# Moving weight loads to GpSimd, u's copy to TensorE, and the last output in two parts, in a planned RWKV-and-MLP kernel

## The chip, the cores and the metric

The kernel runs on one core of a Trainium2 chip. A core has five engines that the texts name as the profile does: PE (TensorE, the matrix engine, with its weight loads as PEld), DVE (the vector engine), ACT (ScalarE), POOL (GpSimd) and SP (which only begins transfers). ACT and POOL can begin transfers too. The core's transfers are carried by 16 DMA engines. The metric is the device time of one execution in microseconds, and the kernel before is given by the median of three of them. "Span" is the time from the first to the last instruction of the one execution that was profiled.

## The reference

Two blocks follow each other. The first is a linear attention with a state of 48x48 per head (4 batches, 8 heads, 768 steps), the second a dense layer with the activation h - tanh(h):

```python
for t in range(S):
    cur = einsum('bhd,bhe->bhde', u[None] * kt, vt)
    y[:, :, t] = einsum('bhd,bhde->bhe', rt, state + cur)
    state = w[None, :, :, None] * state + einsum('bhd,bhe->bhde', kt, vt)
x = y.transpose(0, 2, 1, 3).reshape(3072, 384)
h = x @ w_in            # 384 -> 2048
out = (h - tanh(h)) @ w_out   # 2048 -> 384
```

The inputs r, k, v, w and u are float32, w_in and w_out are float64, which the kernel loads as 64-bit integers and converts to float32 itself. The output is 3072x384 float32.

## The kernel before

**Units.** The sequence is cut into 12 chunks of 64 steps, and each chunk into two halves of two batches: 24 units, each with 128 rows (2 batches by 64 steps) by 8 heads of 48. A unit (`unit(n)` inside `lay_out`) loads r, k and v (two transfers each of 96 KB, begun by SP, for units 0 and 1 half of them by ACT), turns r and k with TensorE (`turn`), scales them by powers of w (`scale_r`, `scale_k`, or `copy_k`), multiplies them into levels (`levels`), masks these into `at` (a predicated copy, L830), forms outputs (`outputs`) and updates the state (`to_state`, `keep`, `decay`). Unit 0 takes u into its levels (`own_k`, `own_levels`); from unit 1 on, the vector engine forms r * k * u (`own`, and L824 with `ub`, a copy of u on all 128 partitions) and its sum `du`. A unit's result goes into `xt` (`to_xt`); a third of it passes through a tile `rest`, from which GpSimd copies it into `xt` by six small transfers per pair of units (`fill`, L786).

**Dense tiles.** Two units make one group of 256 columns, j = 0 to 11. For each group the 2048 hidden numbers are worked through in steps of two times 128 (`hidden`, f = 0, 2, ... 14): `Dense.h` computes h for two blocks of 128 (L217), ACT and the vector engine apply the activation, and `Dense.o` multiplies by w_out (L254), with a form of 7 products in place of 8 for many tiles (`products`, L307, with sums on GpSimd, L290 to L294). The first six groups go in three passes over f; the last six in one, and the last tile of all (group 11, f = 14) is a pass of its own, which ends the kernel: two times `Dense.o`, two adds into `last` (`empty`, L265 and L267), and four transfers to the output at the very end (L1247), two by SP and two by ACT, 96 KB each.

**Weights.** Sixteen pieces (`Weights`): of every four, two of w_in (384 KB of raw numbers in four transfers, 288 KB twice and 96 KB twice) and two of w_out (768 KB in one). Four staging buffers hold raw numbers, so piece n waits until piece n - 4 is converted. In the kernel before, SP begins the large parts and GpSimd the 96 KB parts. Each piece is converted by seven instructions, five on the vector engine (L185 to L191) and two on ACT. Tiles with f = 0 and 2 need pieces 0 and 1 for h and 2 and 3 for o.

**Order.** Nothing is scheduled at run time. `Plan.add` numbers every task in the order in which `lay_out` adds it, and the string `ORDER`, two digits per task in base 64, gives the order in which they are written; each engine then works through its own in that order and waits by semaphores. Numbers behind the last task stand for fills (`fills`, L534): matmuls of the identity whose results nobody reads, put where TensorE would stand idle, and for reading a flag. The first numbers of `ORDER` give TensorE two long fills, the transpose of the columns of w and u (`cols`, L549), two fills more, and then unit 0.

**The start.** w and u come by two small transfers into `rows`. TensorE turns them into columns, the vector engine makes the powers of w and their inverses (L554, L558), and TensorE and ACT make `w_down` from them (L529, L562). `ub` is loaded by one transfer of SP that reads u once for each of the 128 partitions (L568).

Of the kernel before, what the change touches and what calls it, by code (L numbers as in the profile page):

```python
# [10 lines left out]
F32 = mybir.dt.float32  # L11
# [4 lines left out]
ALU = mybir.AluOpType  # L16
# [12 lines left out]
C = 128  # L29
# [5 lines left out]
OWN = 1  # L35
SWAP = 2
# [21 lines left out]
    "AxLo1KLpLqAbB51XB6AoBFA+B71YB8BABG1Z1n1aBT1oBIBJBBAc2G2HBHL31p2FB9L4BUAdBMBKBCBf1bBWAeL5BVAp1cBYBXBNBgBLBaBbAqBi"
    "LTBh1dA_7S23241q2526B01rMABO1sKSKTB1BtBk1yBj1z1tBuB2Bm1+1uBD1_1vBZBE1wBlBvBcBPBy20KxBxBQBwKyKzBnBz2PB_2EC327B+28"
    "C4Bo29BRCH2A21C7BSCIC52BC6C0BdCK22CJCACLBe2XC82CM9MBCMCTCOC92ICN2DBp2J2QBq2RBr2SCUCPMf2TLzMgMhCBChCWCCCVBsCYCiCQ"  # L60
    "CXKdCbC1N3L+CZN4N52UC2CkCj2VCmCDCl2W2KCaCE2LCoCnCt2M2NCuCcD5CFCxCpCwCvCqD6CyCGC+CRD82OD7CzDK2Y2Z2aDL2bCSD92cDADC"
    "CdDBDDC_DZCfDM2dDNCe2eDaCgDECrD0DcDODFCsDbDRDGDdDPDgDoDQ85De86DpDfDS7rD1DrDhDq87EEDTD3DsDUDiEFDtDVDvD2EHDH81DuDW"
    "89ETEIDjEGELEJEUD4DkEK88EiDwEW8AEVDxDIEXEYDJDXEaDy7sDlEjEMENExEk8BElLUEmEy8CEZLVEnEbDYEoEqEzDmEpEOEcEPFNErE_DzE+"
    "FOF0EQF1D+F3DnFQ82FPD_F2EdFSE1EeFTE2FcF4EfFRE3E4E0FdE5EsE6EtE7ERE8FeEBFfE9FUFhESEuFVFgEDFrECFWF5FjEgF6FsEhFtFvEv"
    "FwFXFuFzFYFiEw7zFxEAG4FyF7FZFkG5Fl83F8FmG684G9FnG8F9F+G7FAGWGB7+FBGXFCFDFEFaFFGYGaFGFKGbGlGCGAFLGZF_FbGdFoGmGeGD"
    "FpFHGnFIGqG0G+GoGcG1FMGpG_GfGE7_FqGFH2GsH0FJG280H1GgGtGrG3GGH3H4GhGHGiGJGKGIGLGMHDGNGOGPHEGQGTGSH6GjK5GuH5HHGvGk"
    "HFH7GwHIHfHGGxHJHKH8HgK4H9GVGyHiHAHhHkGzHjHBHlHnHLKVHuK8HvHmK7I7HxHwI8HMKUHyHNHCH_IAHOHzHPHQH+I0HoKEI1IBHpI9IEIM"
    "ICHqKYGRINHrIFLPGUIoKFIOIQKXIDKGIRIPHRIUL6ITIpK+IGISHSIHKHJ1HTHUIIIVI2KIJ2HVIqKJIJIrHsHWL7HXK_HYHtJ4IsKeJ5IWIvIt"
    "IXIuJGKfI3J3I4L1J6I5LOJ7HZIwJHHbJ8HaIxI6JIL2JLKgJJLuJKKKL0JVLWHcJNJMHeJWJ9IyKhJAIKHdKiLQLMJOLXILKmLvKjIzJZL_IZI+"
# [12 lines left out]
    "VJOHWOVqNyWDVrOgOIWCWBP5WPVKVLVMVfVOWQVNW4WEOJVgW5WHVsVuOfOKVtWSORVvWGP6OOOLOQWdP7OMVQP0VRWTW7OPWRW6WFW8WIWeWVWJ"
    "WKOmWfOSWgWLWhVPWsP1WtOnP2OoWvWkWMOpWWWNWUOqWXX5WuWYWwP8WiWZWzWjWaONX6WxP9WlWbX8WmWyW+WnX9PAX7XCW_WcPBXVPCXAXWPD"
    "PIPFXkXYWoXZPHXBWpXlXcPEXXXDX0XzXnXaWqXbXdXEWrXoXFXmX3XGXpX1XqXsXHX+XrX2XtPGYCY0XeX_Y2XfX4Y1YDY4XuY5XgXIYGXvYFXh"
    "XKYRYJYEXwYHY3XJYKYIXLYSXMXNYLXiY6YTYVY7YgYUYWYYYXXOYhXPXSXQXRYvY8YjXTYkY9YiXjYlXxYmYnYMYZXUYwYNYaYOYoXyYxYzYpZ8"
    "YyYbZ0Z9YcYdYAZBY+ZCZYZ1ZAZDYBY_ZZZFYqZ2YrZnZGZcYsZbYPZEZaZHZdYQZeZoZfZ3Z4YeZpZ5ZqZrYfZsa0ZtZuZIZvZJYtZwZgYuZhZ6"
    "Zia1aFa2a5aGa4a3a6a7Z7aJa8aIaUZxaMZyZLZzZKZNZjZOaVa9ZkZPZMZQaXaHZlZRaAaKZSaLZVaNajaYZUaOaWaBabaZakaCZTZWZmalanZ+"
    "aaaPamZXayaQaqaRacazadbIa+b0a_Z_bJb3aeafaDagbLaoapaEarb1asaSb2bKaTbNbMahbObPb4aib5atawb6aubQavaxb7bRb9b8bBbCbAbD"
    "bEbSbFbGbHbUbTbV"
# [104 lines left out]
class Dense:  # L194
# [16 lines left out]
    def h(self, t, z):  # L211
        d = self.d
        if z == 0:
            t.h2 = self.ps_d.tile([128, 2, d.NT], F32, name="h", tag="h")
            t.h = t.h2.rearrange("p z t -> p (z t)")
        for kk in range(d.NK):
            self.nc.tensor.matmul(t.h2[:, z], self.w_in_sb[:, t.f // 2, kk, z * 128 : (z + 1) * 128],  # L217
                                  self.xts[t.j][:, kk].rearrange("p b t -> p (b t)"),
                                  start=kk == 0, stop=kk == d.NK - 1)
# [28 lines left out]
    def o(self, t, half):  # L248

        if t.first and half == 0:  # L250
            self.outs = self.new_outs(t) if self.new_outs else [
                self.ps_d.tile([128, 512], F32, name=f"o{i}", tag=f"o{i}", bufs=1)[:, : self.d.DM] for i in range(L)]
        for z, i in [(0, half), (1, half)] if t.last else [(half, 0), (half, 1)]:
            self.nc.tensor.matmul(self.outs[i], t.g2[:, z, i * C : (i + 1) * C], self.w_out_sb[:, t.f + z, :],  # L254
                                  start=t.first and z == 0, stop=t.last and z == 1)

    def empty(self, t, i):

        whole, at = t.fs[1] == self.d.NF, (t.j, i)
        if t.fs[0]:  # L260
# [134 lines left out]
def near(ctx, tc, r, k, v, w, u, out, shared, moe_w_in, moe_w_out):  # L395
# [135 lines left out]

    def fills(to):
# [7 lines left out]
    def lay_out(early, across_by):  # L540
# [3 lines left out]
        def add(*args, **more):  # L544
# [3 lines left out]
               for e, at, x in (("SP", 0, w), ("ACT", NP, u))]  # L548
        cols = add("PE", .25, lambda: T.transpose(cols_ps, rows.rearrange("p i d -> p (i d)"), ident[: 2 * NP, : 2 * NP]), now)  # L549
# [18 lines left out]
        bonus = add("SP", .65, lambda: Q.dma_start(  # L568
            out=ub.rearrange("p h d -> p (h d)"),
            in_=bass.AP(tensor=u.tensor, offset=u.offset, ap=[[0, 128], [1, H * D]])), data=.7)  # L570
# [39 lines left out]
        def unit(n):  # L610
# [195 lines left out]
            x.turn = None if turned else add("PE", .46, lambda: turn(rt, r_ps), [x.r] + free, steps=8)  # L806
# [74 lines left out]
        def hidden(j, fs, f, due, pace, seven=False):  # L881
# [11 lines left out]
            if m == 0:  # L893
                plan.fills.append(([], now, fills(idle)))
# [385 lines left out]
```

## Time and profile before

| what | value |
|---|---|
| median of three executions | 579.41 us (578.5 to 583.4) |
| the profiled execution | 582.91 us, its span 581.2 us |
| PE busy | 563.5 us, 97% of the span, the fills among it |
| DVE, ACT, POOL busy | 432.1, 404.1 and 202.5 us (74%, 70%, 35%) |
| mean granted TensorE clock | 0.994 |
| moved by DMA | 38.48 MB, 66 GB/s on average |
| last add on DVE | begins at 575.43 us |

Busy time counts each engine's own instructions. The waits that the prediction shows are idle time of an engine, put down to what came last before it went on. A matmul of float32 appears as two instructions. The times in the views count from the span's start, in microseconds.

### The profile page before, as it was taken

To read this page: it belongs to the slowest core of one execution; us is meant where nothing else is said; L and a number is where in the kernel's file an instruction comes from. 1 tells how busy PE (TensorE), PEld (TensorE's weight loads), DVE (VectorE), ACT (ScalarE), POOL (GpSimd) and SP (SyncE) were. 2 spreads that over 40 slices of the span, in tenths; PEclk is the share of its full clock that TensorE was granted. 3 is DMA by queue.
4 is the path that set the end of the run, shared out by engine and by line. 5 is a ranking of instruction groups with operands and counts; after the bars stand their busy time and mean duration, and the time that the engine had idled before them with its cause. 6 is when DMAs were issued, how large, how long until landed. Compare 5 with 4: busy or idle time off the path is not lost.

```text
span 581.2 us, 14164 instructions
## 1 busy us (share of the span) xinstructions
PE 563.5 (97%) x5487; PEld 481.5 (83%) x5487; DVE 432.1 (74%) x720; ACT 404.1 (70%) x926; POOL 202.5 (35%) x366
## 2 busy tenths in 40 slices
PE   7879999999999999999999999999999999999996
PEld 4557777777677789999899899999899898999994
DVE  5789977988999888776888897387685774565435
ACT  2689999998868666455784875766785668666560
POOL 5102211300000146353446355282454263554430
PEclk9899999999999999999999999999999999999998
DMA  8988657446640000032244352442123010010001
GB/s 130 162 204 137 125 100 189 103 76 167 114 120 15 1 1 12 17 55 41 40 74 86 62 94 39 72 86 39 25 50 60 16 34 7 3 29 2 14 16 32
DMA packets 138548, 38.48 MB, mean 66 GB/s; under 512 B 130760, under 2 KB 132904, under 8 KB 138472
## 3 DMA queue, kind: packets, MB, share of 16 engines
q1 hardware_dynamic: 130140, 29.71, 28.1%
q0 software_dynamic: 4992, 6.99, 5.3%
q10 hardware_dynamic: 3340, 0.79, 0.9%
q8 instruction: 45, 0.74, 0.5%
q14 instruction: 31, 0.25, 0.1%
HBM read 31.66 MB, written 4.72 MB: 63 GB/s over the span
## 4 chain that ended last, share of the span: by engine, by line
PE 79%; DMA 1%; ACT 1%; POOL 0%; DVE 0%; issue 0%; DVEq 0%; POOLq 0%
PE h L217 39%; PE p L307 28%; PE o L254 7%; PE yk_ps L606 5%; DMA xt<-rest 1%; PE p L254 0%; ACT xt L765 0%; POOL xt L786 0%; ACT rest L765 0%; ACT kT L692 0%; DVE rk L696 0%; DVE state L792 0%; DVE last L265 0%; PE x_ps L606 0%; DVEq L696 0%
## 5 line engine op out<-in xcount | busy, mean ns | idle before, releaser
L217 PE MATMUL h<-xt,w_in_sb 128*128 128x256 f32 x1152 | 269.0, 381 | 0.4 <-DMA xt<-rest 0.2
L217 PEld LDWEIGHTS h<-xt,w_in_sb 128*128 128x128 f32 x1152 | 214.8, 190 | 33.1 <-DVE w_in_sb L191 0.9
L290 POOL TENSOR_TENSOR sg<-g 128x256 f32<-128x256 f32 x69 | 55.9, 811 | 200.8 <-DVE g L246 147.0
L242 DVE TENSOR_TENSOR g<-h,th 128x512 f32<-128x512 f32 x96 | 65.8, 686 | 61.8 <-ACT tg L233 20.7
L229 ACT ACTIVATE s<-h 128x512 f32<-128x512 f32 x96 | 57.1, 595 | 54.5 <-PE h L217 40.0
L244 DVE TENSOR_TENSOR tg<-s,tg 128x512 f32<-128x512 f32 x96 | 71.7, 751 | 31.2 <-ACT s L224 27.7
L307 PE MATMUL p<-mixed,sg 128*128 128x192 f32 x426 | 93.0, 327 | 0.0
L246 DVE COPY_PREDICATED g<-small,tg 128x512 f32<-128x512 int32 x96 | 74.3, 783 | 12.6 <-ACT small L235 9.9
L231 ACT ACTIVATE th<-h 128x512 f32<-128x512 f32 x96 | 56.8, 593 | 35.0 <-PE h L217 34.7
L307 PEld LDWEIGHTS p<-mixed,sg 128*128 128x128 f32 x426 | 73.5, 190 | 1.4
L233 ACT ACTIVATE tg<-h 128x512 f32<-128x512 f32 x96 | 56.6, 592 | 22.9 <-DVE g L246 13.3
L307 PE MATMUL p<-w_out_sb,g 128*128 128x192 f32 x284 | 69.9, 328 | 0.0
L235 ACT ACTIVATE small<-s,smallb 128x512 f32<-128x512 f32 x96 | 68.5, 720 | 1.2
L254 PE MATMUL o<-w_out_sb,g 128*128 128x384 f32 x192 | 67.2, 489 | 0.1
L224 ACT ACTIVATE s<-s 128x512 f32<-128x512 f32 x96 | 60.1, 630 | 1.1
L786 POOL DMA_DIRECT2D xt<-rest x66 | 32.6, 498 | 68.9 <-ACT rest L765 68.4
L307 PEld LDWEIGHTS p<-w_out_sb,g 128*128 128x128 f32 x284 | 51.1, 190 | 2.7
L254 PEld LDWEIGHTS o<-w_out_sb,g 128*128 128x128 f32 x192 | 35.9, 190 | 19.4 <-issue 0.2
L704 ACT ACTIVATE at<-same,du 128x64 f32<-128x64 f32 x184 | 47.7, 340 | 5.0 <-DVE du L700 4.8
L292 POOL TENSOR_TENSOR sg<-sg,g 128x128 f32<-128x128 f32 x69 | 39.9, 581 | 3.6
L294 POOL TENSOR_TENSOR sg<-sg,g 128x128 f32<-128x128 f32 x69 | 38.1, 559 | 3.0
L307 PE MATMUL p<-w_out_sb,sg 128*128 128x192 f32 x142 | 34.9, 328 | 0.0
(127 smaller groups left out, 653.0 us busy)
## 6 DMA issues: line engine op xcount, KB each, us to landing
st<-in_moe_w_out_dram SPq DMA_DIRECT2D x8, 768.0 KB, 5.5
st<-in_moe_w_in_dram SPq DMA_DIRECT2D x16, 288.0 KB, 5.0
rt<-in_r_dram SPq DMA_DIRECT2D x46, 96.0 KB, 3.4
vt<-in_v_dram SPq DMA_DIRECT2D x46, 96.0 KB, 3.0
kt<-in_k_dram SPq DMA_DIRECT2D x44, 96.0 KB, 3.1
out_dram<-o POOLq DMA_DIRECT2D x44, 96.0 KB, 2.1
st<-in_moe_w_in_dram POOLq DMA_DIRECT2D x16, 96.0 KB, 5.8
parts<-in_k_dram SPq DMA_DIRECT2D x48, 32.0 KB, 2.1
```

Source lines behind the costliest of these rows:

```text
L217: self.nc.tensor.matmul(t.h2[:, z], self.w_in_sb[:, t.f // 2, kk, z * 128 : (z + 1) * 128], self.xts[t.j][:, kk].rearrange("p b t -> p (b ...
L224: A.activation(t.s, t.s, AF.Square, scale=G3)
L229: A.activation(out, t.h, AF.Arctan, scale=G2)
L231: A.activation(out, t.h, AF.Tanh)
L233: A.activation(out, t.h, AF.Tanh, scale=G1)
L235: A.activation(out, t.s, AF.Relu, bias=self.smallb, scale=-1.0)
L242: V.tensor_tensor(t.g, t.h, t.th, ALU.subtract)
L244: V.tensor_tensor(t.tg, t.s, t.tg, ALU.mult)
L246: V.copy_predicated(t.g, t.small.bitcast(I32), t.tg)
L254: self.nc.tensor.matmul(self.outs[i], t.g2[:, z, i * C : (i + 1) * C], self.w_out_sb[:, t.f + z, :], start=t.first and z == 0, stop=t.last ...
L290: add(t.s4[:, :2], g[:, 0::3], g[:, 1:2].to_broadcast([128, 2, C]), ALU.add)
L307: self.nc.tensor.matmul(ps[bank][:, half * n : (half + 1) * n], a, b, start=t.first and half == 0, stop=t.last, skip_group_check=True)
```

## The change

It has five parts. First, u's copy on all partitions is no longer loaded: `spread_u` multiplies the four pairs of rows of u, with a column of the identity spread over 128 columns as the other operand, into a part of unit 1's PSUM bank, and ACT copies it to `ub`. Unit 1's first turn waits for that copy. Second, every transfer of weights from piece 4 on is begun by GpSimd. Third, the first h of tile 0 is computed by units: four tasks, each with 128 columns and half of the rows, in place of two with 256; those of unit 0's columns wait for unit 0 alone. Fourth, the last tile's second output is computed in two parts of 256 and 128 columns, each with its own add; the final transfers are two of 96 KB for batches 0 and 1, as before, and two for batches 2 and 3 together, one of the first 256 columns by ACT and one of the last 128 by SP. Fifth, the whole order is written anew; the fills stand elsewhere, and the small `warm` activation is earlier.

```diff
+LAST = 256
 ...
 ORDER = (
-    "00010J2i2j2k2f2g2h0H2m2l2nbWbW020K030I040605bWbX2q3435362o3231330A2s0F0B0C2r2ubWbX2x072v2y082w2t0T092z0L380M3U3C"
+    "00012m2h2g2i2k2j2l2n2o0Ibbbc020F030L040G0J060A2p0C2r363537050K0B3233342s072t2u380Wbb082v0U2y092z2w393A3V2x3W3X2q"
 ...
-    def h(self, t, z):
+    def h(self, t, z, slot=None):
         d = self.d
+        if slot is not None:
+            if not hasattr(t, "h2"):
+                t.h2 = self.ps_d.tile([128, 2, d.NT], F32, name="h", tag="h")
+                t.h = t.h2.rearrange("p z t -> p (z t)")
+            for kk in range(d.NK):
+                self.nc.tensor.matmul(t.h2[:, z, slot * C : (slot + 1) * C], self.w_in_sb[:, t.f // 2, kk, z * 128 : (z + 1) * 128],
+                                      self.xts[t.j][:, kk, slot], start=kk == 0, stop=kk == d.NK - 1, skip_group_check=True)
+            return
 ...
-    def o(self, t, half):
+    def o(self, t, half, n=None):
 ...
-            self.nc.tensor.matmul(self.outs[i], t.g2[:, z, i * C : (i + 1) * C], self.w_out_sb[:, t.f + z, :],
-                                  start=t.first and z == 0, stop=t.last and z == 1)
+            cols = slice(0, self.d.DM) if n is None else n
+            self.nc.tensor.matmul(self.outs[i][:, cols], t.g2[:, z, i * C : (i + 1) * C], self.w_out_sb[:, t.f + z, cols],
+                                  start=t.first and z == 0, stop=t.last and z == 1, skip_group_check=n is not None)
 ...
+        if n is not None:
+            part = self.sums[at] if n.start == 0 else self.sums.pop(at)
+            a, b, op = (part, self.outs[i], ALU.subtract) if t.j in self.negative else (self.outs[i], part, ALU.add)
+            t.o = self.last[:, i]
+            self.nc.vector.tensor_tensor(t.o[:, n], a[:, n], b[:, n], op)
+            return
 ...
+    ub_ps = x_banks[1][:, 0, : H * D].rearrange("s (h d) -> s h d", h=H)
+    def spread_u():
+        for p in range(NP):
+            put_u = ident[: 2 * NP, NP + p : NP + p + 1].to_broadcast([2 * NP, 128])
+            T.matmul(ub_ps[:, 2 * p : 2 * p + 2], put_u, rows[:, :, :D], start=True, stop=True)
 ...
-        bonus = add("SP", .65, lambda: Q.dma_start(
-            out=ub.rearrange("p h d -> p (h d)"),
-            in_=bass.AP(tensor=u.tensor, offset=u.offset, ap=[[0, 128], [1, H * D]])), data=.7)
+        now = add("PE", .5, spread_u, landed, steps=16)
+        bonus = add("ACT", .5, lambda: A.copy(ub, ub_ps), [now])
 ...
-            queues, data = (("SP",), (3.0,)) if n % 4 > 1 else (("SP", "POOL") * 2, (1.2, .95) * 2)
+            at = "SP" if n < 4 else "POOL"
+            queues, data = ((at,), (3.0,)) if n % 4 > 1 else ((at, "POOL") * 2, (1.2, .95) * 2)
 ...
-            x.turn = None if turned else add("PE", .46, lambda: turn(rt, r_ps), [x.r] + free, steps=8)
+            x.turn = None if turned else add("PE", .46, lambda: turn(rt, r_ps), [x.r] + free + [bonus] * (n == 1), steps=8)
 ...
+            if m == 0:
+                now = add("PE", .66, lambda: dense.h(t, 0, 0), filled[j, "all"][:1] + [converted[piece]], due, steps=12)
+                plan.fills.append(([], now, fills(idle)))
+                now = add("PE", .66, lambda: dense.h(t, 1, 0), [now], due, steps=12)
+                now = add("PE", .66, lambda: dense.h(t, 0, 1), filled[j, "all"] + [now], due, steps=12)
+                plan.fills.append(([flagged], now, fills(tab)))
+                x.h = add("PE", .66, lambda: dense.h(t, 1, 1), [now], due + 1.3, steps=12)
 ...
+            if whole and j == d.NB - 1:
+                x.empty.append(add("DVE", .47, lambda: dense.empty(t, 0), [now], due + 3 * pace))
+                for n, cost, of in ((slice(0, LAST), .87, .38), (slice(LAST, d.DM), .43, .26)):
+                    now = add("PE", cost, lambda n=n: dense.o(t, 1, n), [now] + b1.emptied, due + 2 * pace + 1.3, steps=8)
+                    x.empty.append(add("DVE", of, lambda n=n: dense.empty(t, 1, n), [now, x.empty[-1]], due + 3 * pace))
 ...
-    for b in range(d.B):
-        queue = (nc.sync, nc.scalar)[b % 2]
-        queue.dma_start(out=out[(b + 1) * d.S - SHORT : (b + 1) * d.S, :],
-                        in_=shared["last"][b % 2 * SHORT : (b % 2 + 1) * SHORT, b // 2, :])
+    rows = out.rearrange("(b s) n -> b s n", b=d.B)[:, d.S - SHORT :]
+    for b in range(2):
+        (nc.sync, nc.scalar)[b].dma_start(out=rows[b], in_=last[b * SHORT : (b + 1) * SHORT, 0])
+    for queue, cols in ((nc.scalar, slice(0, LAST)), (nc.sync, slice(LAST, d.DM))):
+        queue.dma_start(out=rows[2:, :, cols], in_=last[:, 1, cols])
```

More of the change, by code (lines that the diff above doesn't have):

```diff
@@ new lines @@
+    "bb2+3C0M3D2_0N300V3H0O3B3T3I3G3S3U0P3J3F3K3E0Q3Lbbbbbc3M3w0D3c0T313N3v3xbc3d0R3O3b3g3s3P0S3Q3t3u3f3R3Y3h8E3i8F3e"
+    "3j3Z3a0X3l404P3k0Y0e448G0Z4Q4R458H4N0a3m4M4O468K3n0b3y473_0c3o410E0d8I423pbf8S163z3+0f434p3q480g4q4r494a0h3r4n4b"
+    "8L4A0i4T4cbfbg4B4W4S4U4d0j4m4o4X4C4w4V5K0k8T4D0m4Y5J5L4Z4H4E4e8O4Lbg4f5G4I0l8M5H5I4G8J4g4K4s8V4J8Nbf4h8U144+8X0x"
+    "8P4x4i4F4v5j4_8Q15504j0v4t4u4y8R4z4k5k5l8W0n510o535U525V8g5h8Z0p8a8h0q545W8Y5g5i8s0r5X8b5N5Y555Q5M5O0s8j6D5R560t"
+    "5P6E6F8t5S576A4l6B6C8c5T5q5C8k585D5n8i5u5A5Z8l5v6d5F8v595B6e6f5w8m8d5E5a0u5x6a8o5b0H8n5mbh5o8e8f8p6b6c5p5c5r8q77"
@@ new lines @@
+    "5s5t6O5d8r6P8u5e8w78796Q5z5y6G746R945+8x5f6H6I8z6S5_6K8y8+6J7Y606o6L7X7Z956p75766q616h6M9G6N6962966g6i668_976T64"
+    "6r677V6890996U7U7W65986k0w9A63136V9B6s1M9C1E6l6W7I6j7J9HJ+7E6X7KK26n9U6mK1K37L9D7A6Y9V9K7i7M6t9J9I9N919X6u9Y179L"
+    "6v7j9W18936Z9Z7D6w7F9c9g9b7B7C7H0y929h0z6xJ_K07G0+726y9E7k6+0_7e707N7a717l1073KO6_9F9M7OKPKQ19117b7c7f9a9O7PKR7m"
+    "6z9P7d7Q129QKu9d1VK57R9R7g1UK4K67h1X7S9iKC7n1A1F9S9u9l7o9k1B9m7p9o9j9T1G9v7q1CKUKVKW9n9e7rKvKw9p1H7zKSKTKDA47y1D"
+    "1I7u7w9f1N9x7v9y1O7x1J1PA51iKx1g9w1K1f9qKyKzA69_1WLJA71h9z9rLILK9+A0A8AI1QK+AB9tAJ1RA99sKEAU1SALKcA1AV1TAMAKA2AC"
@@ L90 @@
+    "aJa7a5a8Yxa9Z9aAaLZlaKaBZmaMaXaCZLZAZMZOZNaPZnZQZRZPZSZTaYZUZVZXZYamaaabaZZoaeaNZWaOaQZZanacaDaRadZ+a_aoafarZ_b0"
+    "aqaga0Zpb3aEasZaa1aFb1b4a2b5b7apaGb2ahatauaibLavajbMaSaTaHbOaUbPaVbNbQaWbRbTb6akbSb8alawazaxbUayb9a+bAbBbCbEbFbD"
+    "bGbHbVbIbJbKbWbXbZbYba"
 )
@@ L548, in lay_out @@
                for e, at, x in (("SP", 0, w), ("ACT", NP, u))]
+        landed = now
         cols = add("PE", .25, lambda: T.transpose(cols_ps, rows.rearrange("p i d -> p (i d)"), ident[: 2 * NP, : 2 * NP]), now)
@@ L567, in lay_out @@
         flagged = add("DVE", .15, lambda: V.tensor_scalar(shared["flag"], tab[0:1, 0:1], 128 * NP - 0.5, None, ALU.is_lt), [now])
[L568 to L570 removed]
+        plan.at = "ub"
+        now = add("PE", .5, spread_u, landed, steps=16)
+        plan.at = None
+        bonus = add("ACT", .5, lambda: A.copy(ub, ub_ps), [now])
         add("ACT", 1.3, lambda: A.activation(fixed("warm", [128, 1]), shared["one"], AF.Arctan), due=0)
@@ L889, in hidden @@
             piece = f // 4 * 4 + f // 2 % 2
-            now = add("PE", 1.29, lambda: dense.h(t, 0), filled[j, "all"] + [converted[piece], b1.h, b2.s, b2.th, b2.tg, b2.g] + ([flagged] if m == 1 else []), due, steps=12)
-            x.h = add("PE", 1.29, lambda: dense.h(t, 1), [now], due + 1.3, steps=12)
+            if m == 0:
[5 more added lines that the diff above has]
+                x.h = add("PE", .66, lambda: dense.h(t, 1, 1), [now], due + 1.3, steps=12)
+            else:
+                now = add("PE", 1.29, lambda: dense.h(t, 0), filled[j, "all"] + [converted[piece], b1.h, b2.s, b2.th, b2.tg, b2.g] + ([flagged] if m == 1 else []), due, steps=12)
+                x.h = add("PE", 1.29, lambda: dense.h(t, 1), [now], due + 1.3, steps=12)
             last_h[j] = x.h
-            if m == 0:
-                plan.fills.append(([], now, fills(idle)))
             x.s = add("ACT", .48, lambda: dense.act(t, "s"), [x.h, b2.m, b2.small, b1.s])
@@ L917, in hidden @@
                 plan.fills.append(([units[1].cp, units[1].diag], now, fills(x_banks[1][:, 0])))
+            whole = fs[1] == d.NF
+            if whole and j == d.NB - 1:
[3 more added lines that the diff above has]
+                    x.empty.append(add("DVE", of, lambda n=n: dense.empty(t, 1, n), [now, x.empty[-1]], due + 3 * pace))
+                x.o = now
+                return
             x.o = add("PE", 1.3, lambda: dense.o(t, 1), [now] + b1.emptied, due + 2 * pace + 1.3, steps=8)
@@ L920, in hidden @@
                 return
-            whole = fs[1] == d.NF
             for i in range(L):
```

75 lines of the change are left out of this document (31 added, 44 removed).

## The prediction

> **What bounds the kernel now.** I read the page first, then the busy time by stretches, then the waits of the start, then the end in order of time.
>
> ```profile
> span 581.2 us, 14164 instructions
> PE 563.5 (97%) x5487; PEld 481.5 (83%) x5487; DVE 432.1 (74%) x720; ACT 404.1 (70%) x926; POOL 202.5 (35%) x366
> PE   7879999999999999999999999999999999999996
> ...
> PE 79%; DMA 1%; ACT 1%; POOL 0%; DVE 0%; issue 0%; DVEq 0%; POOLq 0%
> ```
>
> ```profile
> 35.00:40.00 5.00, 3.22 (x72) 2.38 (x72) 3.37 (x8) 4.88 (x17) 0.00 (x0) 1.00 0.70 136
> 40.00:50.00 10.00, 8.59 (x219) 6.32 (x218) 9.51 (x16) 9.25 (x27) 3.43 (x7) 1.00 0.79 182
> 50.00:60.00 10.00, 10.00 (x166) 7.79 (x165) 9.93 (x18) 9.86 (x32) 0.00 (x0) 1.00 0.84 134
> ```
>
> After its length each stretch has the busy time of PE, weight loads, DVE, ACT and POOL, the clock, the DMA share and GB/s. From about 50 us on TensorE has no gap worth naming, and no matmul of that part becomes cheaper. So the change can win or lose in three places only: how soon TensorE is saturated with real work (much of its "busy" in the first 48 us is fills), new holes after that, and what follows its last matmul. In both written orders the last fill stands behind unit 4's levels, and the same real work is left after it: arriving there earlier moves all the rest. In before that fill ends at 47.76:
>
> ```profile
> 47.06 0.70 PE L534 MATMUL x_ps<-ident 128*128 128x256 f32 x2
> ```
>
> The start is set by the vector engine with loads behind it. Its waits in the first 50 us (total, times, longest):
>
> ```profile
> DVE rT L660 <- ACT kT L692: 2.1, 2, 1.6
> DVE kT L665 <- PE x_ps L656: 1.2, 2, 1.0
> DVE rk L824 <- DMA ub<-in_u_dram: 1.1, 1, 1.1
> DVE power L185 <- DMA st<-in_moe_w_in_dram: 1.0, 1, 1.0
> ```
>
> The end, in order of time (start, duration), and the rate from 572 to 582 us in forty slices of 0.25 us:
>
> ```profile
> 572.65 2.74 PE L254 MATMUL p<-w_out_sb,g 128*128 128x384 f32 x8
> ...
> 573.61 0.35 DVE L335 TENSOR_TENSOR o<-o,p 128x192 f32<-128x192 f32 x1
> 574.14 0.56 DVE L267 TENSOR_TENSOR last<-p,o 128x384 f32<-128x384 f32 x1 [0.18 <-PE p L254]
> ```
>
> ```profile
> 575.43 0.56 DVE L265 TENSOR_TENSOR last<-o,p 128x384 f32<-128x384 f32 x1 [0.73 <-PE p L254]
> 576.01 0.51 SPq L1247 DMA_DIRECT2D out_dram<-last  x1
> 576.01 0.52 ACTq L1247 DMA_DIRECT2D out_dram<-last  x1
> ```
>
> ```profile
> GB/s 33 0 0 0 0 0 0 66 0 33 0 0 0 0 0 49 215 258 258 39 49 197 271 281 6 0 0 12 39 18 12 0 0 0 0 0 0 0 0 0
> ```
>
> The last add ends at 575.99; the two transfers begun then move their bytes in the slices from 577.25 to 578.0, so 1.25 us after issue, and the span ends 3.2 us later (581.2 - 578.0).
>
> **The change part by part.** *u's copy.* A 192 KB broadcast load leaves SP's queue; four matmuls (eight instructions of 96 columns) and an ACT copy of 128x384 come.
>
> ```profile
> 11.45 0.62 SPq L568 DMA_DIRECT2D ub<-in_u_dram  x1
> 12.43 0.48 ACT L562 COPY w_down<-h 128x384 f32<-128x384 f32 x1 [0.74 <-PE h L529]
> 14.14 0.66 PE L656 MATMUL x_ps<-ident,first_k 128*128 128x128 f32 x4
> ```
>
> ```profile
> 125.75 2.59 PE h L217 x12
> ```
>
> Twelve instructions of 256 columns take 2.59 us, 0.84 ns a column, so the eight take 0.65 us, where fills ran; the copy takes 0.48. On ACT it stands ahead of the copy of the decay columns and of two loads of unit 1, issued some 2 us later for it; unit 1's first turn at 14.14 leaves them time. If that cover fails, unit 1 is late by up to those 2 us. The vector engine's 1.1 us for ub goes, so -1.1.
>
> *Weights on GpSimd.* Pieces 0 to 3 keep their queues, but of piece 1 both of GpSimd's parts now stand ahead of unit 1's small copy, behind whose data the second of them was held:
>
> ```profile
> 13.02 0.76 POOL L171 DMA_DIRECT2D st<-in_moe_w_in_dram  x1
> 20.20 0.26 POOL L739 COPY extra<-vt 128x96 f32<-128x96 f32 x1 [6.43 <-DMA vt<-in_v_dram]
> 20.68 1.01 POOL L171 DMA_DIRECT2D st<-in_moe_w_in_dram  x2 [0.21 <-issue]
> ```
>
> That part goes from 20.68 to about 13.8, and with it the 1.0 us wait for st: -1.0. From piece 4 on, 18 transfers move from SP to GpSimd (12 of 288 KB, 6 of 768 KB).
>
> ```profile
> L171 POOL DMA_DIRECT2D st<-in_moe_w_in_dram x16: 510/526/758, 5.4 to 148.6; - x16
> L171 SPq DMA_DIRECT2D st<-in_moe_w_out_dram x8: 385/524/1673, 27.4 to 164.1; - x8
> ```
>
> ```profile
> L345 POOL DMA_DIRECT2D out_dram<-o x44: 521/552/583, 230.0 to 554.5; - x44
> ```
>
> GpSimd takes 526 ns for one of 48 rows and 552 for one of 64, some 1.6 ns a row, so 0.65 us for 144 rows and about 0.85 for 256: 13 us in all, in a stretch where it mostly sleeps. SP loses 18 times about 0.5 us, and the unit loads queued behind no longer wait for a staging buffer. What is queued behind them now is the small copies into xt of units 5, 7, 9 and 11, for which tile groups 2 to 5 wait: below, as a rival. Here 0.
>
> *Tile 0's first h by units.* Twice the instructions at half the columns, by columns the same 2.59 us; the first half starts without unit 1's columns, in time that was fills. 0.
>
> *Written order.* The first loads of unit 0 are no longer behind a 288 KB weight load on SP, and r is turned first; that may take most of the 1.0 us in which the vector engine waited for x_ps. Against it, fewer fills stand ahead of the first turns, and an idle TensorE turns slower here:
>
> ```profile
> 21.57 1.11 PE L656 MATMUL x_ps<-ident,kw 128*128 128x128 f32 x4 [0.90 <-DVE kw L807]
> ```
>
> ```profile
> 24.00:24.50 0.50, 0.50 (x10) 0.50 1.20 86
> ```
>
> At a granted clock of 0.50 four transposes took 1.11 instead of 0.66 us, 0.45 more; two such steps on the way to unit 0's outputs are +0.9. I take 0 for both and keep the ends. [...]
>
> The start together: -2.1 us, from -3.1 (the 1.0 as well) to +0.9 (ACT's kT, 1.6 us already late, takes the place of what is removed, and two cold steps come).
>
> *The last output.* TensorE's last pair is cut 256 and 128 columns, 0.86 and 0.43 us, with the same end at 575.39. The adds of 192 and 384 columns, 0.35 and 0.56, give 1.1 ns a column, so 0.42 for 256 (575.0 to 575.4, then ACT begins 128 KB) and 0.28 for 128 (575.43 to 575.71, then SP begins 64 KB): the last issue is 0.28 earlier, and less is left to move. But these two transfers name the output as 2 batches by 64 rows, where those of before named 64 rows. If a transfer is dealt to the 16 DMA engines along its outer dimension, as the rates above suggest for 64 rows, these two use 2 engines. No row of before shows a bulk transfer with so small an outer dimension, so I bound it by the rate of one engine:
>
> ```profile
> 31.00:32.00 1.00, 1.00 (x6) 0.83 (x5) 0.97 (x2) 0.00 (x0) 0.00 (x0) 1.00 1.03 409
> 576.00:577.00 1.00, 0.00 (x0) 0.00 (x0) 0.00 (x0) 0.00 (x0) 0.00 (x0) 1.00 0.69 193
> ```
>
> 409 GB/s by 16 engines is 25.6 each, the 281 of the last slice 17.6. 196,608 bytes on two are 98,304 each, 3.8 to 5.6 us, from 576.7 (575.44 + 1.25) to 580.5 to 582.3, against 578.0: +2.5 to +4.3, I take +3.4. On all 16 the last 64 KB would end at about 577.25: -0.75. I take the two engines as likelier, as nothing in the pattern but the 2 stands outside the rows. [...]
>
> **Sum.** -2.1 + 3.4 = +1.3 us: 582.5 for the span of 581.2. The profiled execution took 582.91, 1.71 more than its span, and is at the upper end of the three shown (578.5, 579.41, 583.4); on their median it is 580.7.
>
> **The rivals.** *All engines carry the last transfers.* For it: 96 KB went at 281 GB/s. Then -2.1 - 0.75 = -2.85: 576.6; with the best start 575.6.
>
> *Small copies late behind weights.* Unit 9's copies into xt stand behind four weight transfers, 2.1 MB, on GpSimd's queue:
>
> ```profile
> 94.28 2.87 POOL L786 DMA_DIRECT2D xt<-rest  x6 [14.62 <-ACT rest L765]
> ```
>
> ```profile
> 96.66 4.00 DMA xt<-rest
> ```
>
> This landing is on the chain without slack. Against it: GpSimd slept 14.6 us ahead of these copies, enough for 2.1 MB even at 200 GB/s. If the landing doubles, TensorE stands 4.0 us once: 580.7 + 4.0 = 584.7.
>
> *Slower by a fixed time per row on two engines.* In 576 to 577 us 0.69 of 16 engines for 1 us are 11.0 us for 193 KB, 126 rows of 1,536 bytes: 88 ns a row. If a row costs that whatever its length, 128 rows on each of two engines take 11.3 us, to 588.0: +10.0 - 2.1 = +7.9, 587.3. It passes 1% (+5.8) from 72 ns a row. Against it: at 281 GB/s such rows came every 87 ns with two queues in flight, so shorter ones should take less.
>
> **How the numbers follow.** Chances: the forecast 0.52, all engines 0.25, copies late 0.13, fixed time per row 0.10. Predicted 580.7. Its own range is -3.1 + 2.5 to +0.9 + 4.3, so 578.8 to 584.6; with the all-engines case below and the late copies above, 575.5 to 584.7; the fixed time per row is left out. One per cent, 5.8 us, is what a measurement can tell from no change here, as the three executions differ by 4.9. Faster by that needs the best start, all engines and 2 us more: 0.03. Slower: the fixed time, 0.10, and a little of the late copies: 0.12. The same: 0.85.
>
> **What would show it.** The vector engine's waits for ub and for st gone from the first 50 us, and TensorE without fills from about 45.7 instead of 47.8. In the end's slices a rate of some 35 to 50 GB/s over 4 to 6 us in place of 200 to 280; or, for the first rival, the old rate and an end near 580.4 on this start. A wait of h on xt near 95 us would show the late copies. I am wrong if the start's waits only move to ACT's copies (no gain before 48 us), or if the rate at the end is that of sixteen engines.

## The result, and the profile after

| | before | after |
|---|---|---|
| median | 580.32 us (577.17 to 583.62, 20 executions) | 583.60 us (581.87 to 589.73, 20 executions) |
| ratio, with its 95% interval | | 1.0053 (1.0034 to 1.0071) |
| the profiled execution, its span | 582.91, 581.2 us | 583.27, 581.5 us |

The changed kernel is slower by 0.5%, 3.1 us (2.0 to 4.1 by the interval). That is inside the prediction's range and under the 1% that it called no change; the sum of +1.3 us was too small. As the profiled execution of before lies 2.6 us above its median and that of after near its own, two spans 0.3 us apart hide the difference. So the three stretches are read one by one.

**The start** became shorter. These are the vector engine's longest waits in the first 50 us of the changed kernel but for one of 2.5 us for w's columns, which before has too, with 3.0; those for `ub` and for `st` are gone:

```profile
DVE at L857 <- PE x_ps L633: 1.8, 1, 1.8
DVE state L819 <- ACT rest L792: 1.4, 1, 1.4
DVE rT L687 <- PE x_ps L683: 1.2, 1, 1.2
```

Its last fill, in TensorE's order of time, ends at 44.09 us, 3.7 us before that of the profile shown for before:

```profile
42.96 1.13 PE L558 MATMUL x_ps<-ident 128*128 128x512 f32 x2
```

**The middle** has holes that before had not. TensorE's longest waits from 45 us to the end, and three rows of its order of time; the bracket is the idle time ahead of the row and what ended it:

```profile
PE h L226 <- DVE g L251: 1.5, 3, 0.7
PE yk_ps L633 <- DVE state L819: 0.5, 2, 0.4
```

```profile
409.72 1.56 PE L226 MATMUL h<-xt,w_in_sb 128*128 128x256 f32 x6 [0.60 <-DVE g L251]
...
557.52 2.86 PE L226 MATMUL h<-xt,w_in_sb 128*128 128x256 f32 x12 [0.73 <-DVE g L251]
...
570.29 2.76 PE L264 MATMUL p<-w_out_sb,g 128*128 128x384 f32 x12
```

A tile's h goes into one of two banks, which is free only when the vector engine has formed `g` from the tile two before it. The last matmul ends at 573.05 us, 528.96 us behind the last fill; in before it was 575.39 - 47.76 = 527.63.

**The end**, in slices of 0.25 us from 572 us on:

```profile
GB/s 0 0 0 0 0 0 154 209 314 144 66 25 16 49 49 45 25 20 41 63 6 29 45 49 43 49 47 45 45 43 43 41 0 0 0 0 0 0 0 0
```

The first two transfers run at 140 to 310 GB/s. The last two, with the outer dimension of 2, move from about 574.8 to 580.0 us, at 6 to 63 GB/s in the first slices and at 41 to 49 from 577.5 on. The last two numbers of these rows are the DMA share and GB/s; a share of 0.14 of 16 engines is 2.2 engines:

```profile
578.00:579.00 1.00, 0.00 (x0) 0.00 (x0) 0.00 (x0) 0.00 (x0) 0.00 (x0) 0.50 0.14 46
579.00:580.00 1.00, 0.00 (x0) 0.00 (x0) 0.00 (x0) 0.00 (x0) 0.00 (x0) 0.50 0.14 43
```

45 GB/s on two engines are 22.5 each, between the bounds of 17.6 and 25.6 that the prediction took.

GpSimd's busy time rose by 16.7 us for the 18 transfers that it was given (13 were estimated). From the page:

```profile
PE 564.4 (97%) x5507; PEld 483.8 (83%) x5507; DVE 433.3 (75%) x721; ACT 405.6 (70%) x927; POOL 219.2 (38%) x384
```

### The profile page after: what moved, and what is told of

The parts are those of the page before. It is cut to its first block, busy times and chain, and to the rows that moved or that the text cites. A ratio compares the mean times of both kernels' runs of the same rounds, so it can differ in the third digit from the quotient of the medians.

```text
span 581.5 us, 14181 instructions
## 1 busy us (share of the span) xinstructions
PE 564.4 (97%) x5507; PEld 483.8 (83%) x5507; DVE 433.3 (75%) x721; ACT 405.6 (70%) x927; POOL 219.2 (38%) x384
## 4 chain that ended last, share of the span: by engine, by line
PE 82%; ACT 9%; DVE 6%; issue 2%; POOL 0%; DVEq 0%; ACTq 0%; POOLq 0%
PE h L226 38%; PE p L323 23%; PE o L264 10%; PE yk_ps L633 6%; ACT at L731 2%; PE h L558 1%; PE x_ps L683 1%; DVE g L255 1%; DVE g L251 1%; ACT xt L792 1%; ACT s L238 1%; ACT tg L242 1%; DVE tg L253 1%; PE x_ps L633 1%; ACT rest L792 1%
## 5 line engine op out<-in xcount | busy, mean ns | idle before, releaser
L226 PE MATMUL h<-xt,w_in_sb 128*128 128x256 f32 x1140 | 263.7, 381 | 1.5 <-DVE g L251 1.5
L308 POOL TENSOR_TENSOR sg<-sg,g 128x128 f32<-128x128 f32 x69 | 43.5, 633 | 3.5
L310 POOL TENSOR_TENSOR sg<-sg,g 128x128 f32<-128x128 f32 x69 | 39.1, 572 | 3.3
L361 POOL DMA_DIRECT2D out_dram<-o x44 | 24.1, 549 | 40.1 <-DVE o L351 21.8
```

## The experiments

The times are compared by their ratios to before, which was run beside each; a difference of two ratios is turned into us with 580. Two such ratios can be told apart from about 0.35% on, 2 us. The three stretches come from the profile of each kernel: the end of the last fill, from there to the end of the last matmul, and from there to the end of the span.

| kernel | time, us | ratio to before (95%) | last fill ends | to last matmul | to the span's end |
|---|---|---|---|---|---|
| before (shown above) | 580.32 | | 47.76 | 527.6 | 5.8 |
| before, again | 579.46 (one) | | 46.15 | 527.2 | 4.3 |
| after | 583.60 | 1.0053 (1.0034 to 1.0071) | 44.09 | 529.0 | 8.4 |
| after, end as before | 580.69 | 1.0012 (0.9990 to 1.0034) | 44.29 | 529.0 | 4.3 |
| before, changed end | 583.30 | 1.0041 (1.0018 to 1.0064) | 46.85 | 526.9 | 8.1 |
| after, last transfers by rows | 581.26 | 0.9999 (0.9977 to 1.0021) | 45.42 | 529.0 | 6.1 |
| changed start, rest as before | 578.03 | 0.9950 (0.9925 to 0.9975) | 43.98 | 526.7 | 5.5 |
| the same, weights on GpSimd | 578.06 | 0.9947 (0.9921 to 0.9972) | 44.30 | 526.6 | 6.0 |
| the same, last transfers by rows | 578.71 | 0.9958 (0.9927 to 0.9988) | 46.05 | 526.7 | 5.5 |
| after, end as before, g first | 579.26 | 0.9981 (0.9950 to 1.0012) | 44.13 | 527.1 | 5.7 |
| after, end as before, u by a load | 581.73 | 1.0010 (0.9983 to 1.0037) | 45.46 | 528.9 | 6.0 |
| after, end as before, copy first | 580.89 | 0.9993 (0.9968 to 1.0018) | 48.24 | 529.0 | 5.8 |
| the same, again | 581.51 (one) | | 45.03 | 529.0 | 5.7 |
| after, end as before, h whole | 581.66 | 1.0024 (1.0000 to 1.0048) | 46.27 | 529.0 | 4.4 |

### The end

First the changed kernel with the four final transfers as before:

```diff
-    for queue, cols in ((nc.scalar, slice(0, LAST)), (nc.sync, slice(LAST, d.DM))):
-        queue.dma_start(out=rows[2:, :, cols], in_=last[:, 1, cols])
+    for b in range(2):
+        (nc.sync, nc.scalar)[b].dma_start(out=rows[2 + b], in_=last[b * SHORT : (b + 1) * SHORT, 1])
```

> The changed kernel with the four final transfers as before (one of 64 rows by 384 columns for each batch, by SP and ACT in turn); the last tile's product and adds stay in two parts, everything else stays as changed. Two-engine theory: the last bytes move at over 200 GB/s again and not at 45, and the time from the last add to the end of the span goes from 7.8 us (581.5 - 573.7) to the 5.2 us of before (581.2 - 576.0): 2.6 us less than the changed kernel, about 581.0. Rival, that the loss lies in the new written order after the start and the transfers are hidden or too small to matter: within 0.7 us of the changed kernel, 583.6.

The ratio falls from 1.0053 to 1.0012, by 2.4 us. Its slices from 572 us on:

```profile
GB/s 33 0 0 0 0 0 0 172 209 357 82 0 104 227 307 213 0 0 0 0 0 33 0 0 0 0 0 0 0 0 0 0 0 0 0 0 0 0 0 0
```

The last bytes have moved by 576.0. Then the reverse, before with only the two transfers over both batches (its adds stay whole):

```diff
-    for b in range(d.B):
-        queue = (nc.sync, nc.scalar)[b % 2]
 ...
+    for queue, cols in ((nc.scalar, slice(0, 256)), (nc.sync, slice(256, d.DM))):
+        queue.dma_start(out=rows[2:, :, cols], in_=last[:, 1, cols])
```

> The kernel before with only the final transfers of the change (two for batches 2 and 3 together, 256 columns by ACT, 128 by SP; both after the one add). Two-engine theory: 192 KB at some 45 GB/s are 4.4 us where before took 0.75; 3.6 us more, of which up to 1.7 may lie over the 3.2 us that before spends after its last bytes: 1.9 to 3.6 us slower than before. Rival (all engines carry them, the 45 GB/s of the changed kernel come from something else): within 0.5 us of before.

It is slower than before by 2.4 us (1.0 to 3.7), with the rate of the changed kernel:

```profile
GB/s 66 0 33 0 0 0 0 0 0 166 197 350 107 0 14 102 45 41 45 37 8 12 70 49 41 47 49 49 49 49 45 49 49 33 0 0 0 0 0 0
```

So the two transfers cost 2.4 us in either kernel. Whether their outer dimension or their short rows do it is told apart by cutting them by batch: same rows, four transfers, an outer dimension of 64.

```diff
     for queue, cols in ((nc.scalar, slice(0, LAST)), (nc.sync, slice(LAST, d.DM))):
-        queue.dma_start(out=rows[2:, :, cols], in_=last[:, 1, cols])
+        for b in range(2):
+            queue.dma_start(out=rows[2 + b, :, cols], in_=last[b * SHORT : (b + 1) * SHORT, 1, cols])
```

> The changed kernel with its two adds of 256 and 128 columns and its columns kept, but each of the two last transfers cut by batch: four of 64 rows, 64 KB (256 columns) by ACT and 32 KB (128 columns) by SP. Rows are as short as in the changed kernel, the outer dimension is 64 in place of 2. Theory A (the outer dimension sets the number of engines): at the end's slices 150 to 300 GB/s in place of 45, the span ends 3.5 to 4.5 us after the last add in place of 7.8, about 580.5 to 581 us in place of 583.6. Theory B (short rows cost a fixed time each, whatever the engines): about 100 GB/s or less, the span ends 5.5 us or more after the last add, 582.5 us or more.

```profile
GB/s 0 0 0 66 0 33 0 0 0 0 0 37 227 228 289 39 111 197 103 242 146 31 0 0 4 41 8 4 0 0 0 0 0 0 0 0 0 0 0 0
```

The same rows now move at 100 to 240 GB/s: the outer dimension sets the rate, not the length of the rows. The ratio is 0.9999, 3.1 us under the changed kernel; the median, 581.26, is a little above the 580.5 to 581 expected, and the span ends 5.4 us after the last add (575.08), not 3.5 to 4.5: in the slow slices between 578.0 and 579.0 the last eight rows of the output move, see the last section.

### The middle

The changed order up to its last fill, before's order behind it, all weights on SP, and the end as before:

```diff
-ORDER = (the changed order)
+ORDER = (the changed order's first 218 numbers, then the rest as before has them)
-            at = "SP" if n < 4 else "POOL"
+            at = "SP"
```

> The changed kernel with its written order only up to its last fill (44 us); all tasks after that in the order of before, all weights from SP as before, and the four final transfers as before. So the new start with the old rest. Theory A, the start is worth its 3.7 us (last fill ends at 44.1 in place of 47.8) in every execution: 3.7 to 4.0 us faster than before, about 576.5. Theory B, the profiled execution of before was a late one (582.9 against a median of 580.3) and it was late in the start: about 1.0 to 1.5 us faster than before, 579. In both the 1.3 us that the changed kernel loses between its last fill and its last matmul (528.96 against 527.63) is gone if the written order of the rest makes it.

578.03 us, 2.9 under before (1.5 to 4.4), a value between the two expectations. Against the changed kernel with the same end it is faster by 0.6%, and its stretch from last fill to last matmul is shorter by 2.3 us. Two parts of the change were undone in that middle, the order and the queue of the weights. The second kernel puts the weights back on GpSimd:

> This is the kernel with the changed order up to its last fill, before's order behind it and the four final transfers of 64 rows (578.0 us; last fill ends at 43.98, 526.66 us from there to the end of the last matmul), with one thing more: from piece 4 on GpSimd begins all weights, as in the changed kernel. Theory A (the 2 us lost in the middle come from the new written order, where the vector engine or ACT frees a bank of h too late; GpSimd's begins cost nothing): 526.4 to 527.1 us from last fill to last matmul, about 578 us. Theory B (they come from GpSimd's queue, where begins of weights and small copies wait for each other): 528 to 529 us, about 580 us.

578.06 us and 526.64 us from fill to last matmul (43.17 + 1.13 to 568.18 + 2.76):

```profile
43.17 1.13 PE L558 MATMUL x_ps<-ident 128*128 128x512 f32 x2
...
568.18 2.76 PE L264 MATMUL p<-w_out_sb,g 128*128 128x384 f32 x12
```

Theory A: GpSimd's begins cost nothing, the order does. Which tasks, the trace shows. This is the vector engine of the changed kernel ahead of the hole at 409.1 us:

```profile
405.52 0.73 DVE L255 COPY_PREDICATED g<-small,tg 128x512 f32<-128x512 int32 x1
406.14 0.70 DVE L707 STREAM_TRANSPOSE kT<-parts 128x512 f32<-128x512 f32 x1
406.87 0.80 DVE L708 TENSOR_TENSOR kT<-kT,inverse 128x512 f32<-128x512 f32 x1
407.59 0.70 DVE L707 STREAM_TRANSPOSE rT<-parts 128x512 f32<-128x512 f32 x1
408.32 0.74 DVE L708 TENSOR_TENSOR rT<-rT,power 128x512 f32<-128x512 f32 x1
408.99 1.49 DVE L251 TENSOR_TENSOR g<-h,th 128x512 f32<-128x512 f32 x2
```

The four instructions for unit 20, 2.9 us, stand in the written order ahead of the g of tile (8, 2), whose bank TensorE wants. Near 557 us ACT computes th of tile (11, 10) behind three activations of the next tile. The experiment moves three tasks and nothing else:

```diff
 on DVE:  t(8,2).cp of the tile before, 
+         t(8,2).g,
          u20 across_k, u20 across_r,
-         t(8,2).g
 on ACT:  t(11,10).tg,
+         t(11,10).th,
          t(11,12).tg, t(11,10).small, t(11,12).s, t(11,12).sq, t(11,12).small,
-         t(11,10).th
 and g of tile (11,10) on DVE with it
```

> The changed kernel with the four final transfers as before, and three of its tasks moved in the written order: g of tile (8, 2) ahead of the two turned scalings of unit 20 on the vector engine, and th and g of tile (11, 10) ahead of the next tile's activations on ACT. Nothing is added or removed. Theory A (the late holes are the vector engine or ACT doing other work ahead of the g that frees the bank): of the waits of h for g, 1.5 us in the changed kernel, at most 0.3 us are left, 527.6 us from last fill to last matmul in place of 528.97, and about 579.4 us in place of 580.7. Theory B (TensorE is short of work there for another reason, and the holes move): the 528.9 us and 580.7 us stay.

```profile
PE yk_ps L633 <- DVE state L819: 0.6, 2, 0.4
PE x_ps L683 <- issue: 0.3, 1, 0.3
PE yk_ps L633 <- DVE at L857: 0.2, 1, 0.2
PE h L226 <- DVE g L251: 0.2, 1, 0.2
```

The wait for g falls from 1.5 to 0.2 us, the stretch from 528.97 to 527.14 (1.8 less, of which 1.3 are the holes) and the ratio by 0.3%, also 1.8 us. The intervals of these two ratios overlap, so the time alone would not decide; the stretch does, as it is 528.9 to 529.0 in every other kernel with the changed order.

### The start

u by a load again, its matmuls and ACT's copy taken out:

```diff
-        now = add("PE", .5, spread_u, landed, steps=16)
-        bonus = add("ACT", .5, lambda: A.copy(ub, ub_ps), [now])
+        bonus = add("SP", .65, lambda: Q.dma_start(
+            out=ub.rearrange("p h d -> p (h d)"),
+            in_=bass.AP(tensor=u.tensor, offset=u.offset, ap=[[0, 128], [1, H * D]])), data=.7)
```

> The changed kernel with the four final transfers as before, and u's copy again by one broadcast load of SP, behind unit 1's first load of r; the four matmuls and ACT's copy are gone and unit 1's turn doesn't wait for them. Theory A (the prediction's: the load comes too late by about 1 us for the vector engine): a wait of rk for ub of about 1 us is back, the last fill ends at 45.3 in place of 44.29, about 581.7 us in place of 580.7. Theory B (the four matmuls take 2.0 us at the slow clock ahead of unit 0's turns, about as much as the late load costs): the last fill ends at 44.0 to 44.6 and the time stays within 0.5 us.

The last fill ends at 45.46, 1.2 later, the size of theory A; the ratios, 1.0010 and 1.0012, don't tell the two apart. The mechanism of theory A was not seen: no wait of rk for `ub` is in this profile. Two instructions of the vector engine in this kernel, then the same two in the kernel that it is compared with:

```profile
9.06 0.69 DVE L689 TENSOR_TENSOR rT<-x_ps,power 128x512 f32<-128x512 f32 x1 [1.45 <-PE x_ps L685]
23.44 0.56 DVE L725 TENSOR_TENSOR rk<-rt,kt 128x384 f32<-128x384 f32 x1 [1.02 <-DMA rt<-in_r_dram]
```

```profile
8.52 0.69 DVE L687 TENSOR_TENSOR rT<-x_ps,power 128x512 f32<-128x512 f32 x1 [0.90 <-PE x_ps L683]
22.71 0.56 DVE L723 TENSOR_TENSOR rk<-rt,kt 128x384 f32<-128x384 f32 x1 [0.96 <-DMA rt<-in_r_dram]
```

The wait for r at 23 us is about as long in both. Of the 1.2 us, 0.5 are lost by 9 us, at unit 0's first turn, and 0.7 by 23 us. Which part of the edit makes unit 0's turn late, or whether another execution would show it, stays open.

GpSimd's small copy of unit 1 ahead of the second small part of piece 1, as before:

```diff
 on GpSimd: piece 1 part 3,
-           piece 1 part 1,
            unit 1's small copy (thirds),
+           piece 1 part 1
```

> The changed kernel with the four final transfers as before, and on GpSimd the second small part of weight piece 1 again behind unit 1's small copy, as before. Theory A (the prediction's: that part then lands too late by 1 to 2 us): a wait of the vector engine for st of 1 to 2.3 us is back, the last fill ends at 45.3 to 46.3 in place of 44.29, about 582 us in place of 580.7. Theory B (with the new order the piece is wanted later, and other waits end later): the last fill stays at 44.2 to 44.6 and the time within 0.5 us.

The ratio, 0.9993, can't be told from that of the kernel without the edit, and the profiled execution was the latest of twelve, 584.78 us, so that its last fill says little. The same kernel in a second profile:

> The same kernel as the one with GpSimd's small copy of unit 1 ahead of the second small part of piece 1, for one more profile: in the first one the granted clock was 0.50 in two stretches of the start (30 to 32 and 40 to 42 us), which by itself moves its last fill. If the place of that part costs nothing in the new order, an execution without such stretches ends its last fill at 44.2 to 44.8, without a wait for st of over 0.6 us; if it costs what the prediction said, at 45.1 or later.

```profile
DVE power L186 <- issue: 1.2, 1, 1.2
```

The last fill ends at 45.03, 0.7 later than without the edit, between the two expectations and nearer to a cost. L186 is the first conversion of the staging buffer: the wait of 1.2 us is there, though the profile names no DMA for it. So 0.7 us in the profile (0.9 against the changed kernel's 44.09), and not to be told from nothing in the times.

Tile 0's first h in two tasks of 256 columns:

```diff
-                now = add("PE", .66, lambda: dense.h(t, 0, 0), filled[j, "all"][:1] + [converted[piece]], due, steps=12)
+                now = add("PE", .66, lambda: None, filled[j, "all"][:1] + [converted[piece]], due, steps=12)
 ...
-                x.h = add("PE", .66, lambda: dense.h(t, 1, 1), [now], due + 1.3, steps=12)
+                x.h = add("PE", .66, lambda: dense.h(t, 1), [now], due + 1.3, steps=12)
```

> The changed kernel with the four final transfers of 64 rows by 384 columns as before, and tile 0's first h in two tasks of 256 columns, at the places of the two tasks that wait for unit 1; the tasks by units are empty. Theory A (the prediction's: the first half lies in time that was fills, worth nothing): the last fill ends within 0.3 us of 44.29 and the time stays at 580.7 within 0.5 us. Theory B (the halves shorten the way from unit 1 to tile 0's activations): the last fill ends 0.6 to 1.3 us later, 581.3 to 582 us.

The ratio is 0.7 us higher, less than can be told; the last fill ends 2.0 us later. First TensorE's order of time in this kernel, then in the kernel with the halves (L219):

```profile
23.51 0.68 PE L633 MATMUL yk_ps<-vt,kw 64*64 64x48 f32 x32
25.62 0.82 PE L633 MATMUL yk_ps<-rT,state 48*64 48x64 f32 x32 [1.43 <-DVE rT L687]
26.15 1.15 PE L633 MATMUL x_ps<-rT,kT 48*64 48x64 f32 x32
27.23 3.95 PE L226 MATMUL h<-xt,w_in_sb 128*128 128x256 f32 x12
```

```profile
24.67 1.60 PE L219 MATMUL h<-xt,w_in_sb 128*128 128x128 f32 x12
26.21 0.69 PE L633 MATMUL yk_ps<-rT,state 48*64 48x64 f32 x32
26.72 0.65 PE L633 MATMUL x_ps<-rT,kT 48*64 48x64 f32 x32
27.30 1.60 PE L219 MATMUL h<-xt,w_in_sb 128*128 128x128 f32 x12
```

The first halves lie in a gap, in which TensorE otherwise stands idle for 1.43 us; and the whole h, behind that gap, took 3.95 us, at a granted clock of 0.50 from 27 to 29 us and 0.77 in the next. The last fill is later than theory B asked. But a fall of the clock comes in some executions of other kernels too, and their starts were 0.7 to 2.1 us longer with one (last section), so how much of the 2.0 us the halves themselves are worth is not shown; the times leave it open too.

### Two more

Before once more, for a second profile of its start, and the best combination so far with the last transfers cut by rows:

> The kernel before once more, for a second profile. If its first profile was late in the start, the last fill ends earlier than 47.8 us, at about 45 to 46, and the rest is as long (527.6 us to the last matmul's end, 5.2 us from the last add to the end). If it was late elsewhere, the last fill ends at 47.8 again and the difference to 582.9 shows behind it.

```profile
DVE power L185 <- DMA st<-in_moe_w_in_dram: 2.3, 1, 2.3
...
DVE rk L824 <- DMA ub<-in_u_dram: 1.0, 1, 1.0
```

Both waits are there again, and the last fill ends at 46.15 instead of 47.76: before's start moves by 1.6 us from one execution to another. The rest is 0.4 us shorter, and the end 1.5 us. The second:

> The kernel with the changed order up to the last fill, before's order behind it and all weights from piece 4 begun by GpSimd (578.06 us), with its end in two parts by four transfers of 64 rows of 256 and 128 columns. If the two parts' earlier first issue counts, 577.5 us; if the second begin on each queue, some 0.5 us behind the first, sets the end, 578.0 to 578.5 us.

Its ratio is 0.9958 against 0.9947: no gain can be seen. Here the begins last until 1.3 us after the last add (574.72 less 573.39), in the kernel that it is compared with until 0.6 us after it (572.15 less 571.60); so the second begin on each queue may be what takes the gain, but that was not tried alone. The two parts of the last output gained nothing in any form that was tried. The kernel with the changed start, before's order behind it and before's final transfers, 578.03 us, is faster than both kernels of this case, by 0.5% against before (0.25 to 0.75%).

## Why the prediction was right, and where it was not

By its sum: start -2.1, middle 0, end +3.4, together +1.3. The runs give, with no fall of the clock recorded behind 8 us on either side, 44.09 - 46.15 = -2.1 for the start; 528.97 less 527.24 (the mean of the three profiles of before's order: 527.6, 527.2, 526.9) = +1.7 for the middle; and +2.4 for the end, from the ratios. That is +2.0, against 3.1 (2.0 to 4.1) measured. The prediction left out 1.7 us in the middle and took the end 1.0 us too large: that these two errors partly cancel is luck.

- **The start, -2.1: the total is right, its parts are not shown to be.** By the last fills, u's copy was priced at -1.1, and undoing it costs 1.2, but no wait for `ub` comes back; half of it is lost at unit 0's first turn already. The part of piece 1 was priced at -1.0; undoing it costs 0.7. Tile 0's h by units was put at 0, "in time that was fills"; it lies in idle time, and undoing it costs up to 2.0, a fall of the clock among it that alone may cost 0.7 to 2.1. Together these are 1.9 to 3.9, against 2.1 gained, so whether they overlap, or the rest of the new order loses there what the prediction also put at 0, stays open. These are single profiles: the start of the changed kernel, left as it is, ends its last fill at 43.98 to 44.30 in five of seven, at 45.42 in one whose clock was at 0.53 from 8 to 19 us, and at 46.05 in one with a fall of the clock. The times can't tell the parts.
- **Weights on GpSimd, 0: right**, 578.06 against 578.03. (A piece of w_in is 768 KB of raw numbers, as its four transfers add up to.) The rival of late small copies falls: among the waits of TensorE that the view of the changed kernel lists, none is for `xt`.
- **The middle, 0: wrong, and the step that failed.** The prediction said that "the same real work is left after it: arriving there earlier moves all the rest", and weighed the written order only in the start. A new order also changes the rest: 1.5 us of holes where h waits for g, 1.7 us in the stretch, and three tasks moved bring 1.8 us back in the profile. The order was in the diff and could have been read there; in which place an engine's list has another unit's work ahead of the g that frees a bank is visible without a run, its price is not.
- **The end, +3.4: the mechanism agrees with the runs, the size was too large.** The last two transfers moved at 45 GB/s, with bytes until 580.0. The outer dimension set the rate: 45 GB/s for 2 and 100 to 240 for 64 with the same rows. That both transfers share the same two engines was the author's estimate, and no record names an engine. The DMA share of 0.14 agrees with it, and so do the rows in the trace: two of the 256 are under way at once for 4.1 of the 5.2 us, and never more than four, while of the first two transfers' rows it is up to 19. The mis-sized term is the end of before: the prediction read its last bytes at 578.0 and left 3.2 us behind them to both kernels. But the slow slices from 578.75 to 579.75 in its line are output too, eight late rows of it, the last until 579.66 (last section), and the span ends 1.5 us later. In the changed kernel it ends 1.5 us after the last bytes as well (581.5 - 580.0). So against this profile the last bytes come 2.7 us later after the last matmul (7.0 and 4.3 us), and not 3.4; against before's second profile, whose output is through at 576.0, it is 4.3 us. The ratios, which take many executions, give 2.4.
- **The other rivals.** All engines (576.6) is refuted by the rate. A fixed time per row (587.3) is refuted too: 128 rows on each of two engines between 574.8 and 580.0 are 41 ns a row, not 88.

## What to carry to other kernels

Look at the outer dimension of a store: here 2 moved at some 45 GB/s and 64 at 100 to 240, with the same rows; rows outermost were the better choice, even though they needed more transfers. Where an order is written anew, read it through to the end for each bank that is handed over: which engine frees it, and what stands ahead of that in the engine's list. And undo the parts one by one even when the total is as predicted, since here the errors of the middle and of the end partly cancelled.

## What the runs showed of the hardware that was not expected

**The clock falls to half in the middle of the start, in some executions.** Two stretches of 3.4 us each, in the kernel with the copy first (first profile); the columns are as in the prediction, the third number from the end is the granted clock:

```profile
25.80:29.20 3.40, 1.63 (x67) 1.42 (x68) 2.67 (x6) 2.95 (x8) 0.00 (x0) 0.99 1.08 270
29.20:32.60 3.40, 3.40 (x56) 3.18 (x58) 3.40 (x6) 1.05 (x4) 0.00 (x0) 0.50 0.82 128
```

Six such falls begin behind the first 9 us: two here, one each in before, in before with the changed end, in the kernel with h whole and in the changed start with the last transfers by rows. Each lasted about 3.4 us at a granted clock of 0.50, and TensorE had been busy for 1.4 to 2.0 of the 3.4 us before. But that share alone does not decide it. These are four stretches of before, cut in steps of 3.41 us from the begin and the end of its fall:

```profile
18.09:21.50 3.41, 1.43 (x35) 0.85 (x34) 2.62 (x6) 2.93 (x12) 1.08 (x3) 1.00 1.12 203
21.50:24.91 3.41, 3.35 (x56) 2.80 (x56) 3.38 (x7) 0.49 (x1) 0.70 (x2) 0.50 1.21 146
35.15:38.57 3.42, 1.66 (x7) 1.06 (x6) 1.79 (x5) 3.30 (x13) 0.00 (x0) 1.00 0.68 129
38.57:41.98 3.41, 3.09 (x126) 2.20 (x128) 3.41 (x7) 3.25 (x7) 0.00 (x0) 1.00 0.87 234
```

and this is one of the changed kernel, behind which it did not fall either:

```profile
31.23:34.65 3.42, 1.88 (x7) 1.13 (x6) 2.05 (x4) 3.32 (x9) 0.00 (x0) 1.00 0.69 124
```

Stretches in which TensorE was busy for about half were followed by a fall in six places and not in five others with 1.7 to 2.0 us. The six have 35 to 84 matmul instructions, the five 7 to 33, so it may matter how large the matmuls are; that was not tried. Starts with one fall ended 0.7 to 2.1 us later than the same starts with none: 47.76 and 46.85 against 46.15 in before's start and 46.05 against 43.98 in the changed one; with two falls it was 48.24 against 45.03, in the kernel with the copy first. It may be part of why one kernel's executions differ by 5 us and more. Whether more fills there would prevent it was not tried.

**The last rows of the output come late in most profiles.** In nine of the twelve profiles whose last transfers have an outer dimension of 64, the span ends 5.5 to 6.1 us after the last matmul, in the other three 4.3 or 4.4. The view of the queues of before from 578.2 us on, behind the fast slices, shows what is still to come:

```profile
q1 hardware_dynamic: 5, 0.01, 1.4%
q14 instruction: 1, 0.01, 0.7%
q10 hardware_dynamic: 5, 0.01, 0.6%
```

q1 and q10 carry the output, for SP and for ACT. Of their five packets four are rows of 1,536 bytes, a sixteenth of the 64 rows of each transfer, and one has 4 bytes. In the trace a 16 KB packet of the kind "instruction" runs from 577.84 to 578.81, and these eight rows go from 578.80 to 579.66. In before's second profile the packet begins at 575.90 and the output is through at 576.00; there nothing waits. In eight of the nine late profiles the last eight rows, and no others, start within 0.03 us of the end of such a packet; in the ninth other rows still move then. So one of the 16 engines seems to do the packet first and its share of the output after it; the trace does not name the engine, so this is argued. In all fourteen profiles the span ends 1.4 to 1.7 us after the last row of the output. What the packet brings was not tried. In the changed kernel it runs from 574.69 to 575.84, while the slow transfers still have over 4 us to go.
